# Blocks of 128 rows of an expert layer: seven products in pairs on the halves of the array

## The chip, the cores and the metric

The kernel runs on one core of one Trainium2 chip. A core has TensorE (PE, matrix products; PEld are its weight loads), VectorE (DVE), ScalarE (ACT), GpSimd (POOL), SyncE (SP) and 16 DMA engines. The metric is device time in microseconds (us) of one execution. All operands are float32. The trace shows two matmuls and two weight loads for each float32 matmul that the program writes.

## What is computed

Attention with a causal window of 64 on 8 batches of 8 heads, 576 rows and 64 columns, gives 4608 rows x of 512. Each row then goes through one of eight experts, chosen from its logits and its local gate:

```python
for b in range(B):
    prev_e = -1
    for s in range(S):
        fresh_e = int(np.argmax(logits[b, s]))
        if s == 0 or local_gate[b, s] < 0.5:
            e = fresh_e
        else:
            e = prev_e if prev_e >= 0 else fresh_e
        prev_e = e
        ls = logits[b, s] - logits[b, s].max()
        p = np.exp(ls)
        p /= p.sum() + 1e-09
        h = np.maximum(x[b, s] @ w1[e], 0.0)
        out[b, s] = p[e] * (h @ w2[e])
```

An expert has w1 of 512 x 1024 and w2 of 1024 x 512. How many rows an expert gets depends on the data.

## The kernel before

The attention comes first, and its rows go to a DRAM table; the first matmul of an expert (L1514) stands at 134.2 us of the profile. Routing gives each row a place in a block that belongs to one expert. There are four kinds of block: big ones of 256 rows (two slots of 128), small ones of 128 (one slot), halves of 64 and quarters of 32. `run` (L1590) works through a fixed list: three first blocks of 256, and then blocks 0 to 12 of 256 with four small ones behind blocks 1, 3, 5 and 7, a half one behind block 9, another at the end, and two quarters behind blocks 2 and 6. `more` (L1684) handles what is left over with other data.

A block has two layers. `hidden` (L1498) makes h = relu(x w1), transposed, `result` (L1534) makes y = h w2, times the row's probability. From the third of the first blocks on, every engine runs its instructions in the order in which the code writes them; nothing is rescheduled.

- **Plain form** (small, half, and quarter blocks). Small: `hidden` has 32 matmuls of 128x128 weights with 128 moving rows (L1514), in two groups of 512 columns, relu on ScalarE (L1527) and on VectorE (L1525). `result` has eight matmuls with 512 moving columns (L1566), one scaling copy on ScalarE (L1573), and a scatter of the rows by GpSimd. A half block has outputs of 64 columns, which go to the two halves of the array in turn (L1514, L1544).
- **Form of seven products** (big blocks). `big_hidden` (L1344) and `big_result` (L1398) cut both operands into 2 x 2 quarters. Seven products of quarters or of sums of quarters, added up, replace eight. VectorE makes the sums: `prepare` (L1294) four of x (tile `xs`, L1326) and four of w1 (`ws`, L1312); `prepare2` (L1333) four of w2 (`ws`, L1326); `halves` (L1338) four of h (`hs`, L1312). Three products of layer one are kept by ScalarE copies (`keep`, L1370); three adds on VectorE (L1375) and four relu on ScalarE (L1376) give the quarters of h. In layer two L1420 keeps, L1425 adds, L1447 scales the last quarter.

In `big_hidden` the products use three PSUM tiles `px`, `py`, `pz`; the fifth product's `px` is read by VectorE's second add, and the seventh product then goes on in `px`, so it has to wait for that add.

Order around a block i: weights for block i+2 and gathers of rows for block i+3 are asked for; `hidden(i)`, with `prepare2(i)` first on VectorE; `turn(i+1)` (L1268), which transposes the next block's x on VectorE (L1283) and, if the next block has the form of seven products, calls `prepare(i+1)`; `result(i)`, where the callbacks `hooks` put the rest of the next block's weight sums between its products. The tiles of sums exist once each (`bufs=1`), so `prepare2(i)` waits for the last product of `result(i-1)`. `pace` (L1194) ties each of GpSimd's gathers to a product. A block's last scatter is left for the next block (`late`). Two output tiles `y` are used in turn.

## Time and profile before

| | before |
|---|---|
| three runs | 626.38 us median (626.19 to 627.47) |
| profiled execution | 627.78 us |
| its span | 626.0 us |
| granted TensorE clock | 0.999 |
| DMA | 165.80 MB, mean 265 GB/s |

A profile's page has the busy time of each engine, and views group or list the instructions. In a row of the timeline stand start and length in us, engine, line, operation, output <- inputs, stationary or output shape, count, and in brackets how long the engine had been idle and what ended that. In a table of windows stand start:end, length, then for PE, PEld, DVE, ACT and POOL the busy time with the number of instructions, and at the end clock, DMA share and GB/s. A length counts to the result's arrival; instructions of one engine overlap, so that what each costs in a row is the distance of the starts.

### The profile page before, as it was taken

The numbers are of one execution on the slowest core, as the hardware profiler recorded it, in microseconds if no ns is written. First come the engines' busy times: TensorE is split into PE (matmuls) and PEld (weight loads), VectorE is DVE, ScalarE is ACT, GpSimd is POOL, SyncE is SP. The second block draws the span as 40 slices with busy tenths as digits, with TensorE's granted clock in tenths as the row PEclk, the third lists the DMA queues.
The fourth block names the chain that finished last, engine by engine and source line by source line (L and its number), as shares of the span: only waits on it lengthen the run. The fifth ranks groups of instructions, "written<-read, shape, count | busy, mean of one in ns | idle before, by whom it ended". The sixth has DMA issues, their size and how long they took to land. (4 is left out here: it accounts for less than half of the span.)

```text
span 626.0 us, 15072 instructions
## 1 busy us (share of the span) xinstructions
PE 600.5 (96%) x6253; PEld 528.9 (84%) x6253; DVE 403.2 (64%) x757; ACT 200.5 (32%) x368; POOL 271.4 (43%) x261
## 2 busy tenths in 40 slices
PE   7888988999999999999999999999999999999995
PEld 6677766788889999979899799978997998999994
DVE  6567579888996767347381885183926763886730
ACT  3766755722382232203130123112221322123120
POOL 4432111622102567437146775175275866452001
PEclk9999999999999999999999999999999999999999
DMA  8999998787945557476967866687768656955601
GB/s 328 401 415 407 365 378 284 273 304 250 385 153 186 190 210 281 170 272 246 394 245 259 321 198 217 230 314 300 299 239 316 256 189 223 403 193 208 233 18 40
DMA packets 31880, 165.80 MB, mean 265 GB/s; under 512 B 10531, under 2 KB 12217, under 8 KB 22586
## 3 DMA queue, kind: packets, MB, share of 16 engines
q1 hardware_dynamic: 20394, 135.54, 58.6%
q0 software_dynamic: 11408, 29.20, 13.0%
q8 instruction: 51, 0.84, 0.5%
q14 instruction: 27, 0.22, 0.1%
HBM read 145.52 MB, written 19.59 MB: 264 GB/s over the span
## 5 line engine op out<-in xcount | busy, mean ns | idle before, releaser
L1184 POOL DMA_INDIRECT xg<-xs,g x118 | 134.2, 1138 | 46.0 <-issue 25.3
L1494 POOL DMA_INDIRECT out_dram<-y,idx x36 | 41.1, 1142 | 161.3 <-DVE y L1425 68.5
L1414 PE MATMUL hp<-ws,hs 128*128 128x256 f32 x384 | 88.9, 380 | 0.0
L1414 PEld LDWEIGHTS hp<-ws,hs 128*128 128x128 f32 x384 | 72.5, 190 | 10.9 <-issue 1.2
L1363 PE MATMUL hp<-xs,ws 128*128 128x128 f32 x672 | 79.7, 275 | 0.0
L1363 PEld LDWEIGHTS hp<-xs,ws 128*128 128x128 f32 x672 | 77.3, 192 | 0.1
L1425 DVE SCALAR_TENSOR_TENSOR y<-hp,pws,kept 128x256 f32<-128x256 f32 x48 | 23.2, 482 | 68.2 <-issue 41.2
L1514 PE MATMUL hp<-xt,w 128*64 128x64 f32 (+2 forms) x640 | 66.2, 276 | 0.0
L1514 PEld LDWEIGHTS hp<-xt,w 128*128 128x128 f32 (+1 forms) x640 | 60.8, 170 | 4.1 <-issue 0.7
L1414 PE MATMUL hp<-w,h 128*128 128x256 f32 x256 | 60.5, 379 | 0.0
L1375 DVE TENSOR_TENSOR h<-hp,keep 128x512 f32<-128x512 f32 x42 | 28.6, 689 | 43.9 <-PE hp L1363 43.1
L1363 PEld LDWEIGHTS hp<-xt,w 128*128 128x128 f32 x448 | 53.2, 192 | 2.7 <-issue 2.3
L1363 PE MATMUL hp<-xt,w 128*128 128x128 f32 x448 | 54.7, 275 | 0.0
L394 PEld LDWEIGHTS sp<-w 64*64 64x64 f32 x1296 | 39.1, 135 | 16.2 <-issue 11.2
L1414 PEld LDWEIGHTS hp<-w,h 128*128 128x128 f32 x256 | 47.3, 190 | 5.7
L425 ACT ACTIVATE p<-sp 128x512 f32<-128x512 f32 x72 | 39.1, 596 | 37.1 <-PE sp L394 34.8
L440 PE MATMUL xo<-vb,p 128*64 128x74 f32 (+1 forms) x576 | 44.0, 228 | 6.9 <-DVE x L450 3.0
L394 PE MATMUL sp<-w 64*64 64x128 f32 (+1 forms) x1296 | 45.1, 267 | 5.7 <-issue 4.5
L430 DVE TENSOR_TENSOR p<-p,mask 128x1024 f32<-128x1024 f32 x29 | 35.8, 1235 | 22.4 <-ACT p L425 22.3
L1184 POOL DMA_INDIRECT pws<-xw,gx x40 | 44.3, 1107 | 13.2 <-issue 8.5
L440 PEld LDWEIGHTS xo<-vb,p 128*64 128x64 f32 x576 | 38.3, 136 | 12.6 <-issue 5.2
L1376 ACT ACTIVATE h<-h 128x512 f32<-128x512 f32 x42 | 26.3, 630 | 60.1 <-DVE h L1375 60.1
(287 smaller groups left out, 977.5 us busy)
## 6 DMA issues: line engine op xcount, KB each, us to landing
w<-in_w_dram SPq DMA_DIRECT2D x22, 2048.0 KB, 9.4
w<-in_w1t_dram SPq DMA_DIRECT2D x20, 2048.0 KB, 8.7
w<-in_kq_dram SPq DMA_DIRECT2D x17, 1024.0 KB, 11.2
w<-in_w_dram SPq DMA_DIRECT2D x24, 512.0 KB, 8.5
xs<-x POOLq DMA_DIRECT2D x9, 1024.0 KB, 5.9
va<-in_v_dram SPq DMA_DIRECT2D x5, 1184.0 KB, 7.5
vtt<-in_vt_dram SPq DMA_DIRECT2D x5, 1024.0 KB, 6.2
va<-in_v_dram SPq DMA_DIRECT2D x3, 1040.0 KB, 15.5
```

The costliest lines, as they stand in the source:

```text
L394: nc.tensor.matmul(sp[j][c * WIN:(c + 1) * WIN, a:b], lhsT=kt[h, hp, block * WIN:(block + 1) * WIN], rhs=qt[h, hp, a:b], start=not biased, ...
L425: nc.scalar.activation(p[:, j], sp[j], Act.Exp, scale=DH ** -0.5)
L430: masked.append(nc.vector.tensor_tensor(p, p, m.to_broadcast([P, 2, SC]), op=Alu.mult))
L440: nc.tensor.matmul(xo[par * WIN:(par + 1) * WIN, j, s * VW:s * VW + n], lhsT=p[:, j, b * WIN:(b + 1) * WIN], rhs=w[:, s, 2 * hp + j, :n], ...
L1184: return self.nc.gpsimd.indirect_dma_start(out=out, out_offset=None, in_=table[:rows, :], in_offset=bass.IndirectOffsetOnAxis(ap=idx, axis=0))
L1363: mm = nc.tensor.matmul(out[:, m, :], lhsT=a[:, kk, m * P:(m + 1) * P], rhs=b[:, kk, :], start=start and m + kk == 0, stop=stop and (m, kk ...
L1375: nc.vector.tensor_tensor(o, x, y, op=add)
L1376: nc.scalar.activation(o, x if y is None else o, Act.Relu)
L1414: mm = nc.tensor.matmul(out, lhsT=a[:, m, :], rhs=b[:, m, :], start=start and m == 0, stop=stop and m == FK // 2 - 1, skip_group_check=True)
L1425: nc.vector.scalar_tensor_tensor(o, x, pw[i], y2, Alu.mult, Alu.add)
L1494: return self.nc.gpsimd.indirect_dma_start(out=self.out[:, :], out_offset=bass.IndirectOffsetOnAxis(ap=st["idx"][:, s:s + 1], axis=0), in_ ...
L1514: mm = nc.tensor.matmul(hp[a, i, :], lhsT=st["w1"][:, kk, m * P:(m + 1) * P][:, a], rhs=st["xt"][:, kk, :n], start=(kk == 0), stop=(kk == ...
```

## The change

Small blocks now take the form of seven products in both layers. Quarters are 64 rows wide. In layer one each product is a chain of matmuls with 64 columns of weights, alternating between the array's two halves (output partitions 0 to 63 and 64 to 127). In layer two a new function, `small_result`, runs two products at a time, one on each half, each pair into a PSUM bank of its own. What is to be added across halves is moved by ScalarE copies; VectorE adds with 64 partitions. The probability is applied to the whole of y later, together with the scatter. For the block behind a small one, `turn` and `prepare` move from ahead of `result` into its callbacks.

```diff
@@ -1212,8 +1212,9 @@
             slots = range(2 * n, 2 * n + 2) if n < NB else range(SM0 + n - NB, SM0 + n - NB + 1)
             if n >= KINDS[2]:
                 slots = range(HF0 + n - KINDS[2], HF0 + n - KINDS[2] + 1)
-        st.update(x=[], slots=slots, idx=idx, rows=P, big=len(slots) == 2, fast1=len(slots) == 2 and n not in PLAIN1,
-                  fast2=len(slots) == 2 and n not in PLAIN2)
+        st.update(x=[], slots=slots, idx=idx, rows=P, big=len(slots) == 2, fast1=n < KINDS[1] and n not in PLAIN1,
+                  fast2=n < KINDS[1] and n not in PLAIN2)
+        st["wide"] = P if st["big"] else HF
         if n >= KINDS[2]:
             st.update(quarter=n - KINDS[2], rows=QR)
         elif n >= KINDS[1]:
@@ -1293,7 +1294,8 @@
 
     def prepare(self, st, rest=False):
 
-        st["xq"] = quarters(st["xt"], DK, BIG)
+        c = 2 * st["wide"]
+        st["xq"] = quarters(st["xt"][:, :, :c], DK, c)
         st["xt"] = self.right("xs", st["xq"])
         w = quarters(st["w1"], DK, F)
 
@@ -1327,8 +1329,9 @@
         return t1, t2, t3, t4
 
     def sums(self, name, a):
-        t = self.one.tile([P, 4, a[0][0].shape[1], a[0][0].shape[2]], F32, name=name)
-        return [t[:, i] for i in range(4)]
+        n, c = a[0][0].shape[1:]
+        t = self.one.tile([P, 4, n, max(c, P)], F32, name=name)
+        return [t[:, i, :, :c] for i in range(4)]
 
     def prepare2(self, st, marks=()):
 
@@ -1350,23 +1353,25 @@
 
         nc, add = self.nc, Alu.add
         a, s, b, t = st["wq"], st["ws"], st["xq"], st["xt"]
-        self.prepare2(st)
+        if st["fast2"]:
+            self.prepare2(st)
+        n, c = FK // 2, st["wide"]
         st["h"] = h = self.wk.tile([P, FK, BIG], F32, name="h", bufs=1)
-        st["hq"] = hq = quarters(h, FK, BIG)
-        n = FK // 2
-
-        pz, py, px = (self.ps_h.tile([P, n, P], F32, name="hp") for _ in range(3))
+        st["hq"] = hq = quarters(h[:, :, :2 * c], FK, 2 * c)
+
+        pz, py, px = (self.ps_h.tile([P, n, P], F32, name="hp")[:, :, :c] for _ in range(3))
 
         def product(out, a, b, start=True, stop=True):
             for m in range(n):
                 for kk in range(DK // 2):
-                    mm = nc.tensor.matmul(out[:, m, :], lhsT=a[:, kk, m * P:(m + 1) * P], rhs=b[:, kk, :],
-                                     start=start and m + kk == 0,
-                                     stop=stop and (m, kk) == (n - 1, DK // 2 - 1), skip_group_check=True)
+                    for f in range(0, P, c):
+                        mm = nc.tensor.matmul(out[f:f + c, m, :], lhsT=a[:, kk, m * P + f:m * P + f + c],
+                                              rhs=b[:, kk, :], start=start and m + kk == 0,
+                                              stop=stop and (m, kk) == (n - 1, DK // 2 - 1), skip_group_check=True)
             self.pace(mm)
 
         def keep(i, x):
-            o = self.one.tile([P, n, P], F32, name=f"keep{i}")
+            o = self.one.tile([P, n, P], F32, name=f"keep{i}")[:, :, :c]
             nc.scalar.copy(o, x)
             return o
 
@@ -1393,7 +1398,8 @@
         product(px, a[1][1], t[3], False)
         relu(hq[1][0], px)
         step()
-        self.halves(st)
+        if st["fast2"]:
+            self.halves(st)
 
     def big_result(self, st, hooks):
 
@@ -1449,6 +1455,64 @@
             self.late = lambda: self.scatter(st, 1, y[1])
         else:
             self.scatter(st, 1, y[1])
+
+    def small_result(self, st, hooks):
+
+        nc, add = self.nc, Alu.add
+        hooks = iter(hooks)
+
+        def hook():
+            next(hooks, lambda: None)()
+
+        a, s, b, t = st["ha"], st["hs"], st["w2q"], st["w2t"]
+        w, lo, hi = D // 2, slice(HF), slice(HF, P)
+        r3, r2, r1 = (self.ps_h.tile([P, D], F32, name="hp")[:, :w] for _ in range(3))
+        r4 = self.ps_y.tile([P, D], F32, name="yp")[:, :w // 2]
+        y = self.wk.tile([P, D], F32, name="y")
+        u, v, g = (self.one.tile([P, w], F32, name=f"kept{i}") for i in range(3))
+
+        def both(out, *pairs):
+            for m in range(FK // 2):
+                for part, (x, z) in zip((lo, hi), pairs):
+                    mm = nc.tensor.matmul(out[part], lhsT=x[:, m, :], rhs=z[:, m, :], start=m == 0,
+                                          stop=m == FK // 2 - 1, skip_group_check=True)
+            self.pace(mm)
+
+        def plus(o, x, z):
+            nc.vector.tensor_tensor(o, x, z, op=add)
+
+        both(r1, (a[0][0], b[0][0]), (a[0][1], b[1][0]))
+        nc.scalar.copy(g[lo], r1[hi])
+        nc.scalar.copy(u[lo], r1[lo])
+        plus(y[lo, :w], u[lo], g[lo])
+        hook()
+        both(r2, (s[1], t[1]), (s[2], t[2]))
+        plus(v[lo], r2[lo], u[lo])
+        nc.scalar.copy(y[hi, w:], r2[hi])
+        nc.scalar.copy(g[hi], v[lo])
+        hook()
+        both(r3, (s[3], b[1][1]), (s[0], t[0]))
+        nc.scalar.copy(g[lo], r3[hi])
+        plus(v[hi], y[hi, w:], g[hi])
+        plus(y[hi, w:], r3[hi], v[hi])
+        plus(v[lo], v[lo], g[lo])
+        plus(y[lo, w:], r3[lo], v[lo])
+        hook()
+        both(r4, (a[1][1], t[3][:, :, w // 2:]), (a[1][1], t[3][:, :, :w // 2]))
+        nc.scalar.copy(u[hi, :w // 2], r4[lo])
+        plus(y[hi, :w // 2], r4[hi], v[hi, :w // 2])
+        plus(y[hi, w // 2:w], u[hi, :w // 2], v[hi, w // 2:])
+        for _ in range(3):
+            hook()
+
+        def store():
+            nc.scalar.activation(y, y, Act.Copy, scale=st["pw"][0])
+            return self.scatter(st, 0, y)
+
+        if st.pop("later", None):
+            self.late = store
+        else:
+            store()
 
     def quarter(self, st):
 
@@ -1534,7 +1598,7 @@
     def result(self, st, step, hooks=()):
         nc = self.nc
         if st["fast2"]:
-            return self.big_result(st, hooks)
+            return (self.big_result if st["big"] else self.small_result)(st, hooks)
         if "half" in st:
 
             s, w = st["half"], D // 2
@@ -1670,6 +1734,12 @@
             if i + 1 == len(order):
                 self.result(jobs[i], step)
                 continue
+            if jobs[i]["fast2"] and not jobs[i]["big"]:
+                after, left = jobs[i + 1], []
+                self.result(jobs[i], step, ((lambda: self.turn(after, False, True)),
+                                            (lambda: left.append(self.prepare(after, True))),
+                                            (lambda: None), (lambda: left.pop()())))
+                continue
             more = self.turn(jobs[i + 1], i + 1 < FB, rest=i + 1 >= FB and jobs[i]["fast2"])
             if i + 2 < FB and jobs[i + 1]["fast1"]:
                 self.prepare(jobs[i + 1])
```

The order of VectorE's instructions from the first of layer two's sums of a small block to its h, where before only the plain form's relu stood (in `h`, `xs`, `hs`, `y` and `w` the names above; `ws` with a number is one buffer of weight sums, `hp` a PSUM tile, `kept` and `keep` ScalarE's copies). Before, from the big block's last add to the transposes for the block behind:

```order
L1425 SCALAR_TENSOR_TENSOR y<-hp,pws,kept_3524 128x256
L1525 TENSOR_SCALAR h<-hp 128x4x128
L1283 STREAM_TRANSPOSE xt<-xg 128x4x4x32 x2
L1326 TENSOR_TENSOR xs<-xt 128x256
L1326 TENSOR_TENSOR xs<-xt,xs 128x256
```

Now, VectorE from the same add on:

```order
L1431 SCALAR_TENSOR_TENSOR y<-hp,pws,kept_3532 128x256
L1328 TENSOR_TENSOR ws_3570<-w 128x1024
L1328 TENSOR_TENSOR ws_3570<-w,ws_3570 128x1024
L1328 TENSOR_TENSOR ws_3570<-w 128x1024
L1328 TENSOR_TENSOR ws_3570<-w,ws_3570 128x1024
L1380 TENSOR_TENSOR h<-hp,keep_3596 128x4x64
L1380 TENSOR_TENSOR h<-hp,keep_3617 128x4x64
L1380 TENSOR_TENSOR h<-hp,keep_3636 128x4x64
L1314 TENSOR_TENSOR hs<-h 128x4x64
L1314 TENSOR_TENSOR hs<-hs,h 128x4x64
L1314 TENSOR_TENSOR hs<-h 128x4x64
L1314 TENSOR_TENSOR hs<-h,hs 128x4x64
```

One relu has become four weight sums, three adds and four sums of h. Behind them, VectorE in layer two of the same small block, where the transposes and sums for the next block now stand between the adds of this one:

```order
L1482 TENSOR_TENSOR y<-kept_3723,kept_3725 64x256
L1284 STREAM_TRANSPOSE xt<-xg 128x4x4x32 x2
L1482 TENSOR_TENSOR kept_3724<-hp,kept_3723 64x256
L1328 TENSOR_TENSOR xs<-xt 128x256
L1328 TENSOR_TENSOR xs<-xt,xs 128x256
L1328 TENSOR_TENSOR xs<-xt 128x256
L1328 TENSOR_TENSOR xs<-xt,xs 128x256
L1314 TENSOR_TENSOR ws_3758<-w 128x1024
L1314 TENSOR_TENSOR ws_3758<-ws_3758,w 128x1024
L1482 TENSOR_TENSOR kept_3724<-y,kept_3725 64x256
L1482 TENSOR_TENSOR y<-hp,kept_3724 64x256
L1482 TENSOR_TENSOR kept_3724<-kept_3724,kept_3725 64x256
```

The first add, which has to wait for two ScalarE copies, stands ahead of the transposes; three more adds follow the last row, then the next block's third and fourth weight sums of layer one, then its `prepare2`. TensorE at the same place, before:

```order
L1514 MATMUL hp<-xt,w 128x128 x32
L1566 MATMUL yp<-w,h 128x512 x8
L1363 MATMUL hp<-xt,w 128x128 x8
```

and now:

```order
L1368 MATMUL hp<-xt,w 64x64 x16
L1368 MATMUL hp<-xs,ws_3507 64x64 x32
L1368 MATMUL hp<-xt,w 64x64 x16
L1368 MATMUL hp<-xs,ws_3507 64x64 x16
L1368 MATMUL hp<-xt,ws_3507 64x64 x16
L1368 MATMUL hp<-xs,w 64x64 x16
L1477 MATMUL hp<-w,h 64x256 x8
L1477 MATMUL hp<-ws_3570,hs 64x256 x8
```

The 40 matmuls have become 112 of layer one and 32 of layer two; the first pair of layer two (L1477) reads h alone, and both its products stand ahead of everything that uses `hs`.

## The prediction

> **What bounds the kernel now.** I read the page's head first, then the windows of one block of 128 rows and the block behind it, then TensorE's timeline there.
>
> ```profile
> span 626.0 us, 15072 instructions
> PE 600.5 (96%) x6253; PEld 528.9 (84%) x6253; DVE 403.2 (64%) x757; ACT 200.5 (32%) x368; POOL 271.4 (43%) x261
> 336.03:350.05 14.02, 14.02 (x82) 10.19 (x81) 6.57 (x10) 1.07 (x2) 9.29 (x9) 1.00 0.85 315
> 350.05:374.64 24.59, 24.59 (x170) 23.14 (x168) 19.43 (x26) 6.35 (x11) 18.81 (x17) 1.00 0.69 240
> ```
>
> The reader is to see that TensorE (first figure after the length) is busy for the whole of both stretches at full clock. So TensorE sets the end, and a microsecond taken from it or put into it there is a microsecond of the kernel. VectorE (third) uses 6.57 of 14.02 us in the small block but 19.43 of 24.59 in the big one behind it.
>
> ```profile
> 267.96 7.31 PE L1514 MATMUL hp<-xt,w 128*128 128x128 f32 x64
> ...
> 336.03 7.31 PE L1514 MATMUL hp<-xt,w 128*128 128x128 f32 x64
> 343.18 7.03 PE L1566 MATMUL yp<-w,h 128*128 128x512 f32 x16
> 350.05 1.95 PE L1363 MATMUL hp<-xt,w 128*128 128x128 f32 x16
> ...
> 360.76 1.95 PE L1363 MATMUL hp<-xs,w 128*128 128x128 f32 x16
> 362.55 1.89 PE L1414 MATMUL hp<-w,h 128*128 128x256 f32 x8
> ...
> L1566 PE MATMUL yp<-w,h 128*128 128x512 f32 x64 | 28.1, 592 | 0.0
> ```
>
> Spacing is read from start to start. The small block takes 343.18 - 336.03 = 7.15 us for layer one and 350.05 - 343.18 = 6.87 us for layer two, 14.02 in all. In the big block behind it six products take 360.76 - 350.05 = 10.71 us (1.785 each) before the seventh. Four blocks of 128 rows run (64 matmuls of L1566 in all, 16 in each), the first from 267.96, each with a big block behind it.
>
> **The change, TensorE alone.** The blocks of 64 rows already run the new form, pairs of 64 columns on the halves:
>
> ```profile
> 528.77 1.89 PE L1414 MATMUL hp<-ws,h 128*128 128x256 f32 x8
> 530.59 3.95 PE L1514 MATMUL hp<-xt,w 128*64 128x64 f32 x128
> 534.37 3.63 PE L1544 MATMUL yp<-w,h 128*64 128x256 f32 x32
> 537.93 2.05 PE L1363 MATMUL hp<-xt,w 128*128 128x128 f32 x16
> 539.82 3.74 PE L1363 MATMUL hp<-xs,ws 128*128 128x128 f32 x32
> ```
>
> One 64-wide matmul costs 3.78 us / 128 = 29.5 ns, one 256-wide 3.56 us / 32 = 111 ns. The trace counts two matmuls for each of the program's (64 for 32 above), so layer one becomes 7 products of 32, 0.945 us each, 6.61 us; layer two becomes three pairs of products of 16 x 111 ns = 1.78 us, and a fourth pair of 16 matmuls 128 wide. That last form has no row; it lies between 29.5 and 111 ns, and I take the straight line, 57 ns, 0.91 us (ends 0.47 and 1.78). Sum 6.61 + 6.25 = 12.86 us against 14.02: **1.16 us less** per block, if nothing waits.
>
> The switch between full and half array is visible: 530.59 comes 0.09 us after 528.77 plus the product's usual 1.73, and the first product after it takes 1.89 for 1.79. I take 0.1 us on each side.
> [...]
>
> **VectorE and ScalarE.** Now the block needs sums of quarters, in place of plain operands. Prices:
>
> ```profile
> 343.38 0.69 DVE L1525 TENSOR_SCALAR h<-hp 128x512 f32<-128x512 f32 x1 [8.32 <-PE hp L1514]
> 343.98 1.29 DVE L1283 STREAM_TRANSPOSE xt<-xg 128x512 f32<-128x512 f32 x2
> 345.31 0.42 DVE L1326 TENSOR_TENSOR xs<-xt 128x256 f32<-128x256 f32 x1
> 345.77 0.42 DVE L1326 TENSOR_TENSOR xs<-xt,xs 128x256 f32<-128x256 f32 x1
> 346.11 0.42 DVE L1326 TENSOR_TENSOR xs<-xt 128x256 f32<-128x256 f32 x1
> 346.78 1.22 DVE L1312 TENSOR_TENSOR ws<-w 128x1024 f32<-128x1024 f32 x1
> 351.45 1.22 DVE L1326 TENSOR_TENSOR ws<-w 128x1024 f32<-128x1024 f32 x1
> 354.98 1.22 DVE L1326 TENSOR_TENSOR ws<-w,ws 128x1024 f32<-128x1024 f32 x1
> 357.46 0.69 DVE L1375 TENSOR_TENSOR h<-hp,keep 128x512 f32<-128x512 f32 x1 [1.26 <-PE hp L1363]
> ```
>
> Before, VectorE idles 8.32 us in the small block, and everything for the next block is done ahead: two transposes 1.33 us, four input sums 1.47 (345.31 to 346.78), four weight sums of layer one 4.67, four of layer two 4.75 (to 356.20). It is free 1.26 us before the next block's fourth product. So the margin is 1.3 us, and the change puts in: four weight sums of each layer (9.4 us), four sums each of x and h, three adds, and eight adds of the result.
>
> The first part is hidden. The small block's x sums and layer-one sums (about 5.7 us) fall into the big block ahead, where VectorE waits:
>
> ```profile
> 331.11 0.48 DVE L1425 SCALAR_TENSOR_TENSOR y<-hp,pws,kept 128x256 f32<-128x256 f32 x1 [4.57 <-issue]
> 334.57 0.48 DVE L1425 SCALAR_TENSOR_TENSOR y<-hp,pws,kept 128x256 f32<-128x256 f32 x1 [1.26 <-PE hp L1414]
> ```
>
> Without that cover they would cost their length; with it only the last y there comes some 1 us later, at the small block's start. The rest isn't hidden. I follow it with t = 0 at the block's first matmul, with these handovers and small pieces:
>
> ```profile
> 374.84 1.23 DVE L1326 TENSOR_TENSOR ws<-w 128x1024 f32<-128x1024 f32 x1 [0.25 <-PE hp L1414]
> 320.72 1.88 DVE L1375 TENSOR_TENSOR h<-hp,keep 128x512 f32<-128x512 f32 x3
> 321.44 1.83 ACT L1376 ACTIVATE h<-h 128x512 f32<-128x512 f32 x3 [4.31 <-DVE h L1375]
> 322.05 2.05 PE L1363 MATMUL hp<-xs,w 128*128 128x128 f32 x16 [0.24 <-DVE h L1375]
> 614.04 0.42 DVE L1525 TENSOR_SCALAR h<-hp 128x256 f32<-128x256 f32 x1 [3.20 <-PE hp L1514]
> L1466 ACT ACTIVATE qh<-yp 128x256 f32<-128x256 f32 x1 | 0.4, 383 | 1.4 <-PE yp L1462 1.4
> ```
>
> VectorE begins 0.20 us after TensorE passes to the next block (374.84 against 374.64, the window's end), an engine sees another's end some 0.04 us later, and 256 elements take 0.42 on VectorE, also out of PSUM, started 0.36 apart (0.46 where one needs the one before), and 0.38 on ScalarE. No row has adds of 64 partitions, or of 4 x 64 strided elements: from half that (if fewer partitions cost less) to half as much again; I take the 256-element rows, the nearest.
>
> Layer one: the layer-two sums run from 0.20 to 4.95; products three and four end at 2.9 and 3.9, so VectorE is late already. Its adds: 4.95 to 5.37, 5.30 to 5.72; the seventh product, which overwrites the second one's source, may start at 5.8, just when the sixth ends. It ends at 6.74, ScalarE's relu of it at 7.35. The first pair of layer two needs this last quarter at once (in the big form the first product does not): **about 0.5 us of wait**. TensorE finishes the first pair at 7.35 + 15 x 0.111 = 9.02. Then two copies on ScalarE (9.22 to 9.94) and VectorE's first add at 9.98; it had finished the four h sums at 8.45 and stands idle meanwhile, because the transposes for the next block are queued behind that add.
>
> From there VectorE never rests: add 0.38 (10.36), transposes 1.33 (11.69), add 0.38 (12.07), x sums 1.48 (13.55), two weight sums 2.4 (15.95), four adds 1.64 and two of 128 elements 0.48 (18.07), two weight sums 2.33 (20.40), four sums of layer two 4.75 (25.15), and the next block's adds, first 25.15 and second 25.75 to 26.44. TensorE ends its pairs at 10.80, 12.58, 13.49, starts the next block at 13.59 with the switch, and is ready for its seventh product at 13.59 + 10.71 = 24.30. That product overwrites what the second add reads: it waits until 26.48, **2.2 us**. Weight sums needed earlier are in time: the first by 14.8 for 15.4, the second by 15.95 for 17.2, the third by 19.3 for 20.7. Behind the waiting seventh product stands the whole layer two; from there on VectorE has its usual lead again (its h sums end 2.1 us after layer two begins, as now).
>
> Before, the same seventh product starts at 14.02 + 10.71 = 24.73. So 26.48 - 24.73 = **+1.75 us** per block, and four times that is +7.0. SyncE's weight loads keep their releases within half a microsecond, and GpSimd's gathers lead by three blocks; I cost both at nothing.
>
> One wait is new: the first add writes a buffer that the big block's first scatter reads.
>
> ```profile
> 267.27 1.01 POOL L1494 DMA_INDIRECT out_dram<-y,idx  x1 [6.26 <-DVE y L1425]
> 276.67 1.01 POOL L1494 DMA_INDIRECT out_dram<-y,idx  x1 [5.52 <-DMA out_dram<-y,idx]
> 338.41 1.02 POOL L1494 DMA_INDIRECT out_dram<-y,idx  x1 [0.30 <-issue]
> 344.55 1.01 POOL L1494 DMA_INDIRECT out_dram<-y,idx  x1 [2.60 <-DMA out_dram<-y,idx]
> ```
>
> The next scatter waited for the first to land, at 276.67 and 344.55. From the blocks' starts at 267.96 and 336.03 that is t = 8.7 and 8.5; the first of these scatters had waited for the last y, and with y 1 us later it lands at 9.7. The add comes at 9.98: covered, with 0.3 us to spare. Where it isn't, VectorE's queue moves by as much; up to 1 us per block goes into the upper end.
>
> The profiled execution is the span of 626.0 plus 1.8 around it, 627.78, 1.40 above the median of the runs shown; 627.78 + 7.0 = 634.8 stands for a median of 626.38 + 7.0 = **633.4 us**.
>
> **Rivals.** (a) VectorE is in time. Ten operations of the queue behind the first pair (9.02 to 26.44, 17.4 us) have no row of their own: two copies of 0.36 and eight adds, 2.9 us. At half price they give 1.8 us, and the change breaks even (it does from 1.75); from 2.2 us on TensorE sets the end, the block gives 24.30 - 24.73 = -0.43, four times -1.7: 624.7. For it: no row has these forms. Against it: 12 us of the queue are sums and transposes that have rows, and the page's short operations (0.42 for 256 elements, 0.69 for 512) show a fixed part of 0.15 that doesn't halve. Chance 0.09, with 0.05 for landing between and within 0.2%, which is about what a measurement can tell from no change (1.25 us).
> (b) The halves do not overlap in layer two, where each has its own weights and its own moving rows. Then a 256-wide matmul costs 0.216 (L1414's 1.73 / 8), layer two some 12.2 us, the seventh product starts at 7.35 + 12.2 + 0.1 + 10.71 = 30.4, +5.6 per block: 648.9. Against it: L1544 has two moving streams and goes at 111 ns. Chance 0.03.
> (c) The scatter lands late in each block, by 2 us after the add's time: +8 more, 641. Chance 0.06.
>
> **How the numbers follow.** The forecast keeps 0.77: +7.0 with the lone unknowns (the 128-wide pair -0.4 to +0.9 per block, but hidden behind VectorE; adds 1 us either way; scatter up to +1) gives 629 to 638. The range 628.5 to 640 leaves out (a) with what lies between it and the forecast, and (b), (c): not quite 2 in 10. Faster by over 0.2% 0.09, within 0.05, slower 0.86.
>
> **What would show it.** The steps, each for four blocks: 64x64 matmuls spaced 29.5 ns and 64x256 111 ns; a gap of about 0.5 us before the first pair of layer two, ended by ScalarE; VectorE without a pause from the first add to the next block's adds; a gap of 2 us before the seventh product of the next block, ended by VectorE's add (now L1380); 13.6 us from a small block's first matmul to the next block's. Wrong if that gap is missing, if the small block itself takes over 14, or if a wait sits elsewhere, as before the second product or at the scatter.

## The result, and the profile after

| | before | after |
|---|---|---|
| time, us (median; lowest to highest) | 626.29 (625.63 to 627.47) | 642.69 (640.20 to 646.11) |
| the profiled execution, us | 627.78 | 642.25 |
| its span, us | 626.0 | 640.5 |
| mean granted clock | 0.999 | 0.991 |

The kernel is slower: ratio 1.0263, 95% interval 1.0213 to 1.0314, or +16.4 us on the median. The prediction had +7.0 and a range of 628.5 to 640.0: the right side, and a time above the range. Ratios, here and below, compare executions in the faster of two states that the cores show; medians and spans are over all that ran.

First the page's head after the change, then the rows of the view of waits in which TensorE waits in the blocks of 128 rows and behind them (total us, times, longest):

```profile
span 640.5 us, 16918 instructions
PE 603.0 (94%) x7085; PEld 535.6 (84%) x7085; DVE 464.9 (73%) x861; ACT 216.2 (34%) x416; POOL 277.2 (43%) x261
...
PE hp L1368 <- DVE h L1380: 9.5, 6, 2.3
PE hp L1368 <- issue: 3.3, 2, 1.7
PEld hp L1477 <- ACT h L1381: 2.1, 4, 0.6
```

TensorE was busy for 96% of the span and is now for 94%: waits have come in. The first row is the predicted one (L1380 is VectorE's add); the third is the predicted half microsecond before the first pair of layer two. The second, "issue", is ended by nothing that the profile shows, and nobody had forecast it.

TensorE's timeline of the second block of 128 rows and the big block behind it answers to the rows of 336.03 to 360.76 shown of before:

```profile
339.01 1.15 PE L1368 MATMUL hp<-xt,w 128*64 128x64 f32 x32
339.99 2.04 PE L1368 MATMUL hp<-xs,ws 128*64 128x64 f32 x64
341.86 1.10 PE L1368 MATMUL hp<-xt,w 128*64 128x64 f32 x32
...
345.59 2.38 PE L1477 MATMUL hp<-w,h 128*64 128x256 f32 x15
...
352.44 2.05 PE L1368 MATMUL hp<-xt,w 128*128 128x128 f32 x16
354.33 3.74 PE L1368 MATMUL hp<-xs,ws 128*128 128x128 f32 x32
...
361.48 1.95 PE L1368 MATMUL hp<-xt,ws 128*128 128x128 f32 x16
365.69 3.42 PE L1368 MATMUL hp<-xs,w 128*128 128x128 f32 x16 [2.26 <-DVE h L1380]
```

The block takes 352.44 - 339.01 = 13.43 us (predicted 13.59, before 14.02), and one product of the new layer one 0.94 us. Then the six products run as ever, and the seventh, which would be ready at 361.48 + 1.79 = 363.27, starts at 365.69: 2.42 us late, of which the row counts 2.26 as idle, since a length runs to the result's arrival. This wait, ended by VectorE, is there in this form behind all four blocks. That product takes 3.42 us, not 2.05.

The first block of 128 rows shows the "issue" wait, in the middle of its last product of layer one:

```profile
270.88 0.74 PE L1368 MATMUL hp<-xs,w 128*64 128x64 f32 x17
273.23 0.62 PE L1368 MATMUL hp<-xs,w 128*64 128x64 f32 x14 [1.60 <-issue]
```

Every operand of that product is ready, since 17 of its matmuls have run. The fourth block has such a wait of 1.70 us; the second and third have none. Layer one takes 8.50 and 8.49 us in the first and fourth block, for 6.58 in the second.

**Where the 14.5 us of span went.** From a small block's first matmul to the seventh product behind it, the four blocks take 28.64, 26.68, 26.78 and 28.58 us, 110.68 in all; before, 4 x 24.73 = 98.92. That is +11.76, of which 3.83 are the two "issue" waits (3.3 us idle; 3.83 by the lengths of layer one) and 7.93 the predicted kind (7.0 forecast). The seventh product and the next one take 5.27, 5.26, 3.61 and 5.28 us for 3.52, **+5.3 us**. Together +17.1, less 2.8 because this execution reached its first small block 2.8 us sooner (265.18, before 267.96): 14.3 of 14.5. Those 2.8 us are luck, in a part that the change doesn't touch; other traces of a calm chip get there at 266.76 to 267.94.

For the slow products I read the granted clock. The windows below are cut to 3.41 us, and to a grid on which the stretches at half clock lie: those begin at 294.44, 366.12 and 506.07, and the distances, 71.68 and 139.95 us, are 21 and 41 times 3.413. Columns: length, busy time of TensorE, its weight loads, VectorE, ScalarE and GpSimd, then the clock, the DMA share and GB/s.

```profile
291.03:294.44 3.41, 1.15 (x10) 0.96 (x10) 3.30 (x5) 1.24 (x3) 2.84 (x2) 1.00 0.24 82
294.44:297.85 3.41, 3.41 (x16) 3.23 (x16) 2.10 (x4) 1.19 (x2) 2.50 (x4) 0.50 0.17 48
362.71:366.12 3.41, 1.15 (x10) 0.96 (x9) 3.38 (x5) 1.05 (x2) 2.80 (x3) 1.00 0.14 38
366.12:369.53 3.41, 3.41 (x17) 3.32 (x16) 2.10 (x4) 1.16 (x3) 2.50 (x4) 0.50 0.20 66
427.57:430.98 3.41, 2.94 (x27) 2.75 (x25) 3.38 (x4) 0.00 (x0) 2.80 (x3) 1.00 0.11 13
430.98:434.39 3.41, 1.62 (x14) 1.62 (x15) 2.68 (x5) 1.82 (x3) 2.80 (x3) 1.00 0.16 55
434.39:437.80 3.41, 3.41 (x19) 3.05 (x19) 3.00 (x9) 1.07 (x2) 2.50 (x4) 1.00 0.75 233
502.66:506.07 3.41, 1.23 (x11) 1.23 (x12) 2.69 (x4) 1.83 (x3) 2.80 (x3) 1.00 0.27 96
506.07:509.48 3.41, 3.41 (x14) 2.96 (x13) 3.27 (x6) 0.60 (x1) 2.80 (x3) 0.50 0.44 101
```

Behind a stretch in which TensorE was busy for 1.15, 1.15 or 1.23 us, the next runs at half clock. In the third block the same wait falls across a border of the grid, TensorE is busy for 2.94 and 1.62 us in the two stretches, and the clock stays at 1.00. So the wait costs its own length and, when it falls badly, some 1.75 us more.

### The profile page after: what moved, and what is told of

Its sections match the earlier page's. It is cut to its first block, busy times and chain, and to the rows that moved or that the text cites. A ratio compares the mean times of both kernels' runs of the same rounds, so it can differ in the third digit from the quotient of the medians.

```text
span 640.5 us, 16918 instructions
## 1 busy us (share of the span) xinstructions
PE 603.0 (94%) x7085; PEld 535.6 (84%) x7085; DVE 464.9 (73%) x861; ACT 216.2 (34%) x416; POOL 277.2 (43%) x261
## 3 DMA queue, kind: packets, MB, share of 16 engines
q0 software_dynamic: 11408, 29.20, 12.9%
## 5 line engine op out<-in xcount | busy, mean ns | idle before, releaser
L1184 POOL DMA_INDIRECT xg<-xs,g x118 | 138.4, 1173 | 42.4 <-issue 25.6
L1368 PE MATMUL hp<-xs,ws 128*128 128x128 f32 (+1 forms) x1056 | 92.3, 256 | 0.0
L1368 PEld LDWEIGHTS hp<-xs,ws 128*128 128x128 f32 (+1 forms) x1056 | 89.2, 172 | 0.1
L1368 PE MATMUL hp<-xt,w 128*128 128x128 f32 (+1 forms) x704 | 64.1, 257 | 0.0
L1368 PEld LDWEIGHTS hp<-xt,w 128*128 128x128 f32 (+1 forms) x704 | 61.0, 172 | 2.8 <-issue 2.4
L1380 DVE TENSOR_TENSOR h<-hp,keep 128x512 f32<-128x512 f32 (+1 forms) x54 | 32.5, 627 | 33.6 <-PE hp L1368 33.5
L1381 ACT ACTIVATE h<-h 128x512 f32<-128x512 f32 (+1 forms) x54 | 30.7, 583 | 77.4 <-DVE h L1380 77.4
L1184 POOL DMA_INDIRECT pws<-xw,gx x40 | 46.3, 1157 | 13.6 <-issue 8.9
L1328 DVE TENSOR_TENSOR ws<-w 128x1024 f32<-128x1024 f32 x40 | 49.0, 1228 | 3.8 <-PE hp L1420 2.5
L1328 DVE TENSOR_TENSOR ws<-w,ws 128x1024 f32<-128x1024 f32 x40 | 49.0, 1224 | 0.7
L394 PE MATMUL sp<-w 64*64 64x128 f32 (+1 forms) x1296 | 42.8, 263 | 4.9 <-issue 3.0
```

The source lines that it names most:

```text
L394: nc.tensor.matmul(sp[j][c * WIN:(c + 1) * WIN, a:b], lhsT=kt[h, hp, block * WIN:(block + 1) * WIN], rhs=qt[h, hp, a:b], start=not biased, ...
L1184: return self.nc.gpsimd.indirect_dma_start(out=out, out_offset=None, in_=table[:rows, :], in_offset=bass.IndirectOffsetOnAxis(ap=idx, axis=0))
L1328: self.nc.vector.tensor_tensor(o, x, y, op=sub)
L1368: mm = nc.tensor.matmul(out[f:f + c, m, :], lhsT=a[:, kk, m * P + f:m * P + f + c], rhs=b[:, kk, :], start=start and m + kk == 0, stop=sto ...
L1380: nc.vector.tensor_tensor(o, x, y, op=add)
L1381: nc.scalar.activation(o, x if y is None else o, Act.Relu)
```

## The experiments

The kernels of one set ran on one chip, each beside the kernel before, and are compared only with what ran there. The chips of the first, second, third and fifth set ran the kernel before in 637.7 to 647.6 us (medians), with waits that the page of before doesn't have, and the changed kernel, where it ran, at ratios of 1.038 to 1.048; the text calls them restless. Only the chip of the fourth set was as calm as that of the result (627.45).

Theory A: VectorE's queue makes the wait, and the wait the halved clock. Rival: the waits that no engine ends (theory B, later theories F and G on their cause) make most of the loss.

### First set: take the wait away, and make one in the old kernel

The changed kernel with the work for the next block at the head of `small_result`, ahead of the adds of the result:

```diff
@@ small_result
+        hook()
+        hook()
         both(r1, (a[0][0], b[0][0]), (a[0][1], b[1][0]))
 ...
         plus(y[lo, :w], u[lo], g[lo])
-        hook()
         both(r2, (s[1], t[1]), (s[2], t[2]))
 ...
-        hook()
```

> The changed kernel with the next block's transposes, x sums and first two weight sums ahead of the small block's adds. Theory (VectorE's queue makes TensorE wait 2.26 us before the seventh product of the next block, and that idle time is what halves the clock afterwards): VectorE's 1.5 us of idle time ahead of the first add goes, the wait shrinks to some 0.7 to 0.9 us, the clock stays at 1.00, and the time falls by 4 x 1.5 + 5.3 = about 11 us against the changed kernel, to some 631. Rival (the clock is lost for a reason that has nothing to do with the wait, such as the switch to half the array or the load of 64-wide matmuls): the wait shrinks, the clock is still lost, about 637. Stalls of 1.7 us inside the 64-wide products, put down to issue, stay in both.

The changed kernel with matmuls that nobody reads, where TensorE would wait (in the big blocks behind the small ones):

```diff
+        if st.get("fill"):
+            spare = self.ps_y.tile([P, D], F32, name="yp")[:, :2 * P]
+            for _ in range(5):
+                nc.tensor.matmul(spare, lhsT=a[1][1][:, 0, :P], rhs=st["w1"][:, 0, :2 * P], start=True, stop=True)
```

> The changed kernel with five matmuls of 256 columns that nobody reads (2.16 us) ahead of the seventh product of each big block behind a small one. Theory (the idle time halves the clock): TensorE has no gap there any more, the seventh product starts where it did (26.7 us after the small block's first matmul), runs in 1.8 us and not 3.1, the clock stays at 1.00 and the time falls by some 5 us, to 637. Rival (the products behind the wait are slow from contention with VectorE or from the 64-wide forms): they stay at 3.1 and 2.2 us, the time stays at 642.

The kernel before with sums that nobody reads on VectorE, in the big blocks behind the small ones, four and five of them:

```diff
+        for _ in range(st.get("extra", 0)):
+            spare = self.one.tile([P, FK // 2, D // 2], F32, name="spare")
+            self.nc.vector.tensor_tensor(spare, w2[0][0], w2[0][1], op=Alu.add)
```

> The kernel before, with four more sums of 128x1024 on VectorE behind the layer-two sums of each big block behind a small one; their result is not used. Four sums are 4.7 us against a margin of 3.2 us at the seventh product: theory, a wait of 1.4 to 1.5 us there in four blocks, no loss of clock, +6 us, 632. Rival (any wait of over a microsecond costs the clock): +6 and up to 1.7 us for each of four, 636 to 639.

> The same with five sums, 5.85 us: a wait of 2.6 us in four blocks. Theory (a wait of some 2.3 us and more halves the clock for 3.4 us in most of the cases): 4 x 2.6 plus 3 or 4 times 1.7 = 15.5 to 17.5 us more, 642 to 644, the granted clock of 0.50 for 3.4 us behind the wait. Rival (the clock loss belongs to the 64-wide forms, which this kernel doesn't have in these blocks): +10.5, 637, clock 1.00.

Measured: e1_reorder 661.85 us, ratio 1.0296 (1.0205 to 1.0387); e2_fill 670.23, 1.0460 (1.0378 to 1.0543); e3_old_4_sums 651.42, 1.0164 (1.0057 to 1.0272); e4_old_5_sums 650.66, 1.0152 (1.0056 to 1.0248). Two rows of the waits of e1_reorder (667.71 us in its profiled execution, the longest of its four) say what became of it:

```profile
PE hp L1368 <- issue: 16.8, 17, 5.8
...
PE hp L1368 <- DVE h L1380: 0.7, 3, 0.3
```

With the work moved, the wait for VectorE falls from 2.26 us to 0.3 at most, and in both e1_reorder and e2_fill the seventh product runs at full clock in all four places (1.8 to 1.9 us to the next product's start). That much theory A expected. But TensorE also came late to these places, by other waits, so the reordering isn't shown here to be the whole reason. A cleaner case is the second place in the later sets: the unaltered kernel waits 2.28 us there in e9_after_third, e16_after_fourth and e18_less (none in e6_after_again), the reordered one 0.90 and 0.91 in e12_reorder_again and e17_reorder_third.

The time does not follow: 631 and 637 us were expected of e1_reorder and e2_fill. That was a miss, and it gave the second question. Of the 16.8 us of "issue" waits in e1_reorder only 6.2 stand inside 64-wide products; 10.3 stand in two places in 128-wide ones, before the third product of the big blocks behind the first and the third small one (e2_fill: 6.7 and 5.6 of 12.4). The first of the two, and ScalarE at the same time:

```profile
294.19 3.78 PE L1368 MATMUL hp<-xs,ws 128*128 128x128 f32 x16 [4.48 <-issue]
...
293.55 0.59 ACT L1375 COPY keep<-hp 128x512 f32<-128x512 f32 x1 [4.05 <-remote]
```

The third product goes on in the PSUM tile that this copy reads, and it starts 0.05 us behind the copy's end (294.14). So this is a wait for ScalarE that the profile puts down to "issue"; ScalarE itself had stood still for 4.05 us, released by "remote", a semaphore whose sender the profile doesn't show. The other one (5.81 us, at 443.50) ends 0.05 us behind such a copy too, and so, within 0.06 us, do the longest waits in 128-wide products of e2_fill, e12_reorder_again, e16_after_fourth and e17_reorder_third (2.2 to 4.4 us). In the result's profiled execution ScalarE has no such stop.

The old kernel's form brings the clock's fall too. The seventh product at the third of the four places, with four sums and then with five (timeline):

```profile
436.46 2.05 PE L1366 MATMUL hp<-xs,w 128*128 128x128 f32 x16 [1.47 <-DVE h L1378]
```

```profile
436.81 3.25 PE L1366 MATMUL hp<-xs,w 128*128 128x128 f32 x16 [2.71 <-DVE h L1378]
```

and the grid's stretches with five sums, two at the third place and two at the fourth:

```profile
434.01:437.42 3.41, 0.70 (x6) 0.61 (x6) 3.31 (x5) 1.22 (x3) 2.58 (x3) 1.00 0.25 82
437.43:440.84 3.41, 3.41 (x16) 3.23 (x16) 2.07 (x4) 1.19 (x2) 1.69 (x3) 0.50 0.17 38
505.69:509.10 3.41, 2.05 (x19) 1.86 (x17) 3.34 (x3) 0.00 (x0) 2.58 (x3) 1.00 0.33 115
509.11:512.52 3.41, 2.02 (x17) 2.02 (x18) 2.68 (x6) 1.82 (x3) 1.89 (x2) 1.00 0.23 41
```

Four waits of 2.70 to 2.76 us: the one that lies in a single stretch of the grid (busy 0.70) halves the clock, the one that is split (2.05 and 2.02) doesn't, nor do the other two, and four waits of 1.44 to 1.47 never do. No 64-wide products run there, so they are not what brings the clock down. One case of four is fewer than the three or four expected, and the times don't show the price: the two kernels measured the same (651.42 and 650.66 us, two executions each, 632 and 642 to 644 expected), with more "issue" waits in e3_old_4_sums (2.1 us for 0.6). What a lost clock costs rests on the traces.

### Second set: is it the form, and is it the traffic

> The kernel before, profiled beside the others on the chip that this call gets. The chip of the first experiments needed 643 us for it, where 626 stood before: theory (late instruction fetches, seen as waits for issue and as ScalarE standing still without a semaphore), waits of this kind of 10 us and more on TensorE's way on such a chip, hardly any on one that needs 626. Rival (a lower clock or slower operations): the same operations are longer throughout.

> The changed kernel again. Theory: the wait before the seventh product of the big block behind each small one is 2.26 us again in all four places, the clock halves for 3.4 us behind some of them, and the waits for issue inside the 64-wide products come at other places and in other numbers than in the first profile, between 0 and 4 blocks, more of them where the kernel before is slow too. Rival (the waits for issue belong to fixed instructions): blocks one and four again, 1.6 and 1.7 us.

The changed kernel with SyncE's loads of the next block's layer-two weights held back until the last matmul of the small block's layer one:

```diff
+                if end:
+                    self.tc.add_manual_dep(d.ins, end.ins.name, ...
 ...
+            if i >= FB and small:
+                self.weights(jobs[i + 1], order[i + 1], ("w2", ), end=jobs[i]["end"])
+                self.weights(jobs[i + 2], order[i + 2])
```

> The changed kernel with the load of the next block's second weights (2 MB) held back until the small block's layer one is done, so that the DMA engines carry little beside gathers while the 64-wide products run. Theory (instruction fetches come late because the DMA engines are full): no wait for issue inside the 64-wide products, layer one in 6.6 us in all four blocks, 3 us less than the changed kernel where that has two such waits. Rival (the sequencer itself cannot keep up with 64-wide products): they stay.

Layer one by the change, layer two as before:

```diff
-                  fast2=n < KINDS[1] and n not in PLAIN2)
+                  fast2=len(slots) == 2 and n not in PLAIN2)
```

> Layer one of the small blocks in the new form, layer two as before. VectorE has no layer-two sums, h sums and adds to make there, so it is done with the next block's sums about 8 us after layer one ends. Theory: no wait before the next seventh product, clock 1.00, small block 6.6 + 6.9 + 0.2 = 13.7 us against 14.0, -1.3 in all, and waits for issue as in the changed kernel, 0 to 4 times 1.7, so 625 to 632 against 626. Rival (layer one alone already overloads VectorE): a wait of a microsecond or more before the next block's seventh product.

Measured: the kernel before once more, 640.45 us in one execution (median there 637.73); e6_after_again 666.95, ratio 1.0478 (1.0425 to 1.0531); e7_quiet 676.35, 1.0579 (1.0511 to 1.0648); e8_layer1 662.18, 1.0408 (1.0351 to 1.0465). In e5_before_again the clock (0.999) and the lengths of the operations are those of before (L1414: 1.89 us for eight matmuls in both timelines), so the chip's loss lies in waits; of "issue" waits in the expert blocks it has 3.4 us, not 10. The "issue" waits at L1368, the line of both forms, are 11.1, 7.1 (there L1371) and 10.7 us in the other three; 7.3, 6.4 and 8.6 of them stand in 64-wide products. In e7_quiet the DMA engines are nearly idle while the second block's layer one runs (from 351.22 us; share 0.20 from 350 to 364 us, 0.84 in e6_after_again in the same stretch), and the short waits are there in both, more of them in e7_quiet, so busy DMA engines are not their cause. e7_quiet also waits 11.6 us for ScalarE before layer two of the small blocks (0.6 in e6_after_again); ScalarE itself stood still there twice, 8.5 us in all, released by "remote", so it isn't shown that holding the weights back did it. Layer one alone keeps most of the loss.

### Third set: layer two alone, and the form alone in the old kernel

> The changed kernel once more, beside the next three on one chip. Theory A (VectorE's queue and the clock behind it): a wait for VectorE of about 2.2 us before the seventh product of each of the four big blocks, a granted clock near 0.5 for some 3.4 us behind most of them, 3.5 to 5.3 us in all lost by it; waits that no engine ends inside the 64-wide products add from 3 (first measurement) to 11 us (second) on top. Ratio to the kernel before 1.025 to 1.05.

```diff
-                  ... fast1=n < KINDS[1] and n not in PLAIN1,
+                  ... fast1=len(slots) == 2 and n not in PLAIN1,
```

> Layer two of the four blocks as changed, layer one as before: 128x128 matmuls, no 64x64 ones. Theory B (the waits that no engine ends belong to the 64-wide matmuls of layer one): they are gone, under 2 us in all. The rival (they belong to the whole stretch, whatever TensorE does there): 7 us or more, as in the changed kernel. VectorE's queue behind the first pair keeps its length, so both expect the wait of 2 to 3 us before the seventh product, and by theory A a granted clock near 0.5 behind it in some of the four. By A and B together: four times (2.5 us of wait, 0.7 of gain by layer two) is +7, with 0 to 7 for the clock: ratio 1.011 to 1.022. By the rival 1.025 or more.

The kernel before, layer one of the four blocks cut into 64x64 pieces (its values there then differ from the reference's; the amount of work is as told):

```diff
-                    for f in range(0, P, st["rows"]):
-                        a = slice(f, f + st["rows"])
-                        mm = nc.tensor.matmul(hp[a, i, :], lhsT=st["w1"][:, kk, m * P:(m + 1) * P][:, a],
-                                         rhs=st["xt"][:, kk, :n], ...
+                    c, z = (HF, HF) if n == P else (st["rows"], n)
+                    for f in range(0, P, c):
+                        for r in range(0, n, z):
+                            mm = nc.tensor.matmul(hp[f:f + c, i, r:r + z], lhsT=st["w1"][:, kk, m * P + f:m * P + f + c],
+                                             rhs=st["xt"][:, kk, r:r + z], ...
```

> The kernel before with layer one of its four blocks cut into 64x64 matmuls on the quarters of the array, 128 in the program where 32 were, and nothing else: no sums, no products by seven, no new wait. At 29.5 ns each of the 256 that the trace counts, layer one takes 7.55 us for 7.15: +0.4 per block, +1.6 in all, ratio 1.0026. Theory B (waits inside runs of 64-wide matmuls that no engine ends): these come here too, some 60 ns for each instruction in stretches, 5 to 15 us in all, ratio 1.01 to 1.025. If they stay away, the form alone doesn't bring them, and something beside it does (operands that VectorE has just made, or its own traffic).

> The changed kernel with the transposes, the input sums and the first two weight sums for the next block ahead of the adds of the small block's result, where VectorE stood still. By theory A the wait before the seventh product goes (below 0.4 us) and the clock behind it stays at 1.00: 4 x 2.26 + 4 x 1.5 = up to 15 us less than the changed kernel on the same chip, ratio to the kernel before 1.00 to 1.01. If the waits that no engine ends decide instead (theory B), the time moves by less than 5 us from the changed kernel's and these waits take 10 us or more.

Measured: e9_after_third 674.73, ratio 1.0411 (1.0348 to 1.0473); e10_layer2 652.06, 1.0102 (1.0036 to 1.0169); e11_old_quarters 655.12, 1.0133 (1.0076 to 1.0190); e12_reorder_again 674.39, 1.0347 (1.0267 to 1.0427).

Layer two alone has no "issue" waits in these blocks, and keeps the others: 2.30 and 2.41 us for VectorE before the seventh product in the second and fourth big block, with half clock behind each, 0.88 in the third, none in the first, and new ones of 1.91 and 1.12 us for ScalarE before a third product, and of 3.11 for VectorE in the big block ahead of the fourth. It gains nothing either: its blocks take 14.3 to 15.5 us, where layer one's values now leave through two engines and the first pair waits for them (for VectorE 1.8 us in the four blocks). The form alone, without sums or new order, brings "issue" waits into 64-wide products of the old kernel (11.0 us): theory B holds for these, not for the ones in 128-wide products, which e11_old_quarters doesn't have in layer one of the big blocks behind the small ones. e12_reorder_again is a second miss for A: the waits for VectorE before the seventh product are down to 1.6 us, and the ratio is not clear of that of e9_after_third (the intervals overlap), where up to 15 us less had been expected. On this chip TensorE lost so much earlier in the blocks that VectorE was in time at some places anyway (4.3 us of waits for it in e9_after_third, 9.5 in the result).

### Fourth set, on a calm chip: the rate of instructions, and GpSimd

The same edit over halves only, so 64 columns of weights by 128 moving columns:

```diff
+                    c = HF if n == P else st["rows"]
+                    for f in range(0, P, c):
+                        mm = nc.tensor.matmul(hp[f:f + c, i, :], lhsT=st["w1"][:, kk, m * P + f:m * P + f + c],
+                                         rhs=st["xt"][:, kk, :n], ...
```

> The kernel before with layer one of its four blocks cut over the halves only: 64 columns of weights, 128 moving columns, 64 matmuls in the program where 32 were and e11_old_quarters had 128; nothing else. If the waits that no engine ends come from the rate at which TensorE takes its instructions (theory B), half the rate leaves little of them: below 4 us in the four blocks, layer one 7.2 to 7.6 us, ratio to before below 1.006. If they come from any use of the array's parts, or from the stretch itself, they stay near the 14 us of e11_old_quarters and the ratio is 1.01 or more.

e11_old_quarters with one gather for a block:

```diff
-            if st["plain"]:
+            if n < KINDS[1]:
                 asks.append((x, self.xs, gx[:, s:s + 1], rows))
```

> e11_old_quarters with one gather of whole rows on GpSimd for each block of 128 rows, where four gathers of quarter rows were (the rows then stand in another order in the block, so what layer one is given differs; the work of TensorE, VectorE and ScalarE is the same). If GpSimd's backlog of gathers, which is longest in the second and fourth block, is what the 64-wide matmuls meet (theory G), their waits fall from 14 to below 4 us and the ratio from 1.013 to below 1.005. If not, 8 us or more remain, and the two worst blocks stay the second and the fourth.

> e11_old_quarters once more, on the chip of the two runs above: ratio 1.007 to 1.02, waits that no engine ends inside its 64-wide matmuls of 8 to 16 us. Below 5 us here would say that they belong to the chip, and the two runs above can then tell nothing.

Measured: e13_old_halves 627.00 us, ratio 0.9999 (0.9972 to 1.0026); e14_one_gather 636.25, 1.0134 (1.0089 to 1.0180); e15_quarters_again 636.33, 1.0126 (1.0068 to 1.0184). Layer one of the first and third block in the timeline of e13_old_halves:

```profile
266.76 7.21 PE L1514 MATMUL hp<-xt,w 128*64 128x128 f32 x128
...
398.36 7.21 PE L1514 MATMUL hp<-xt,w 128*64 128x128 f32 x128
```

and in e15_quarters_again:

```profile
267.94 6.34 PE L1515 MATMUL hp<-xt,w 128*64 128x64 f32 x209
276.03 1.62 PE L1515 MATMUL hp<-xt,w 128*64 128x64 f32 x47 [1.75 <-issue]
...
402.58 4.93 PE L1515 MATMUL hp<-xt,w 128*64 128x64 f32 x160
410.42 4.41 PE L1515 MATMUL hp<-xt,w 128*64 128x64 f32 x96 [2.91 <-issue]
```

The same work in half as many instructions runs without a wait; in twice as many it stops (6.5 us in all, less than the 8 to 16 expected, at the expected ratio). The 4.41 us of the last row hold a clock halved from 410.10 on, behind a wait that no VectorE ended. TensorE stops behind 209 matmuls in the first block, 160 in the third and 214 in the fourth. e14_one_gather stops behind the same 209, 160 and 214, with GpSimd busy for 171.0 us instead of 269.2, so theory G falls, though its waits (5.5 us) are below the 8 us that had been named for that. e11_old_quarters, on another chip, stopped behind 209 and 160 too. A wait that stands at a place in the instruction stream, whatever the chip and the traffic, points to the stream itself: theory F, TensorE's instructions arrive late. The DMA view lists instruction packets (q8 is a queue; in the page after the change 58 packets and 0.95 MB, 16 KB each). In the changed kernel's first measurement a single one of 16 KB starts between 268 and 274 us, in the window from 270.84 to 270.86 (packets, MB, share of the 16 engines in that window):

```profile
q8 instruction: 1, 0.02, 292.5%
```

| kernel, place | TensorE's last matmul | the packet, from to | TensorE goes on | behind the landing |
|---|---|---|---|---|
| after, first block | 271.40 | 270.85 to 271.79 | 273.23 | 1.44 |
| after, fourth | 481.03 | 480.58 to 481.57 | 482.95 | 1.38 |
| e15_quarters_again, first | 274.06 | 273.68 to 274.56 | 276.03 | 1.47 |
| e15_quarters_again, third | 407.29 | 408.18 to 409.12 | 410.42 | 1.30 |
| e15_quarters_again, fourth | 482.17 | 481.80 to 482.72 | 484.18 | 1.46 |
| e16_after_fourth, first | 276.76 | 276.41 to 277.35 | 278.64 | 1.29 |

Each wait ends 1.3 to 1.5 us behind the landing of one 16 KB packet, which started within 0.9 us of TensorE's last matmul. The places can be counted in the traces, with the queue's semaphore instructions. From the first to the third block's wait of e15_quarters_again TensorE's queue runs 2560 instructions (1265 matmuls, 1266 weight loads, 29 semaphores), and 1536 from there to the fourth block's; the two waits of the changed kernel lie 4096 apart: exactly 5, 3 and 8 times 512. And in every trace that has the first block's wait, of the old kernel and of the changed one, it stands behind the 7617th instruction of that queue.

### Fifth set: the two causes together

e16_after_fourth is the changed kernel and e17_reorder_third is e1_reorder, unaltered. e18_less was to leave out one sum:

```diff
+            if NB <= n < KINDS[1]:
+                jobs[i + 1]["less"] = 1
             more = self.turn(jobs[i + 1], i + 1 < FB, rest=i + 1 >= FB and jobs[i]["fast2"])
```

> The changed kernel, as the measure for the next two on one chip. Theory A: a wait for VectorE of 2.2 to 2.3 us before the seventh product of all four big blocks, and the granted clock halved for 3.4 us behind those whose TensorE idle time in one stretch of the clock's grid (3.41 us) is above 1.9 us, at full behind those below 1.85. Theory F (instruction fetch): waits of 1.3 to 1.9 us inside the 64-wide products of the first and the fourth block, at the same matmuls as in the first measurement (after 17 of the seventh product's, and in the sixth product), each ending 1.3 to 1.6 us behind the landing of a 16 KB instruction packet. Ratio 1.02 to 1.03 on a chip as calm as the first.

> The changed kernel with the transposes, the input sums and two weight sums for the next block ahead of the adds of the small block's result. Theory A: waits for VectorE's add before the seventh product at most 0.4 us, clock 1.00 behind them, so 4 x 1.9 to 2.26 + 3.5 to 5.3 = 11 to 14 us less than e16_after_fourth on this chip: ratio to before 1.000 to 1.007. Theory F: TensorE's instructions are the same, so the waits for instructions stay where they are. The rival (only the waits that no engine ends count): no more than 4 us less than e16_after_fourth.

> The changed kernel with the last of the four layer-two weight sums left out in the big block behind each small one (the third stands in its place, so those blocks' results differ). VectorE's queue is 1.19 us shorter there: theory A expects the wait before the seventh product at 2.26 - 1.19 = 1.05 to 1.1 us in all four, too short for the clock: 1.00 behind all four. So 4 x 1.19 + 3.5 to 5.3 = 8 to 10 us less than e16_after_fourth. The rival for the clock (the 64-wide products bring it down, not the wait) expects 0.50 behind the waits as before and only 4 to 5 us less.

Measured: 668.78 us, ratio 1.0376 (1.0282 to 1.0470); 671.10, 1.0441 (1.0338 to 1.0543); 672.17, 1.0424 (1.0320 to 1.0529). The edit of e18_less stands behind a branch that these blocks don't take, so VectorE runs the same 861 instructions, and the run is only one more of the changed kernel: a failed experiment, and the direct test of a shortened wait was not made. The wait behind the 17th matmul of the first block's seventh product is in all three (1.65, 1.49 and 1.70 us), as theory F expected, and in every other run whose layer one has the new form (in e8_layer1 behind the 16th, at the same count of the queue) but e7_quiet, where the packet lands at 278.77, before TensorE gets there. The wait in the fourth block, which theory F expected too, is in none of the three. e17_reorder_third is the third miss for A on a restless chip: only one wait for VectorE is left there that is longer than half a microsecond (0.91 us), e16_after_fourth has only one (2.28 us), and 14.5 and 12.9 us of "issue" waits at L1368, about half of them (7.8 and 6.8) in 128-wide products, hide the rest.

## Why the prediction came out too low

**Right, by its own steps.** The products of layer one take 0.94 us each for 0.945 forecast. The first pair waits for ScalarE, 2.1 us over four blocks, forecast 0.5 each. VectorE's first add of the result starts 10.06 us into the second block for 9.98, and from there it runs without a pause to the next block's adds:

```profile
349.07 0.42 DVE L1482 TENSOR_TENSOR y<-kept,kept 64x256 f32<-64x256 f32 x1 [1.73 <-ACT kept L1486]
349.41 1.29 DVE L1284 STREAM_TRANSPOSE xt<-xg 128x512 f32<-128x512 f32 x2
...
363.10 1.22 DVE L1328 TENSOR_TENSOR ws<-w,ws 128x1024 f32<-128x1024 f32 x1
364.35 1.89 DVE L1380 TENSOR_TENSOR h<-hp,keep 128x512 f32<-128x512 f32 x3
```

The seventh product starts 26.68 and 26.78 us into the second and third block, forecast 26.48, and 26.72 and 26.67 into the first and fourth when the "issue" waits are taken off. That is 0.2 to 0.3 us a block too late, 0.9 in all: the sum's small prices were that far off. In all four places the wait is ended by the add that was named, and where the reordering could be compared, at the second place, it is shorter (0.9 us for 2.28), so its cause is the one named. Rival (a), VectorE in time, and (b), halves that don't overlap, are out; so is (c), since no wait for the scatter stands before that add, only ScalarE's 1.73 us.

**Wrong, first: the step from one block's loss to four times it.** The prediction counted the wait at its own length, +1.75 a block, and let everything behind it run at the usual pace, "from there on VectorE has its usual lead again". VectorE had; the clock hadn't. Three of the four waits lie in one stretch of the clock's grid and are followed by half clock (0.50) for the next 3.41 us: **+5.3 us**. That of the third block is split and costs nothing more. e4_old_5_sums shows the same in a kernel without the change (busy for 0.70 us of a stretch, the next at 0.50). Why the clock falls there, and what sets the grid, no run shows. The page before had no such case, since no wait of TensorE's in its expert blocks comes near this length (the longest is 0.4 us); the clock at 1.00 in its windows was taken for granted.

**Wrong, second: the step "TensorE alone".** 29.5 ns for a 64-wide matmul came from a run of 128 of them (530.59), in which the DMA view of before has no instruction packet. In layer one there are now 224 traced matmuls where 64 were, and in the first and the fourth block TensorE stands there for 1.6 and 1.7 us, until 1.44 and 1.38 us behind the landing of an instruction packet: **+3.8 us** in the first measurement, by the lengths of layer one. That fetch is the cause of these two waits is inferred from their places (the 7617th instruction of the queue in the first block, 4096 from there to the fourth), from the packets' landings, and from the half rate, without such a wait in e13_old_halves; no run changed the fetch itself. Why the packet starts so late, and why some blocks have none, was not tried.

Without either one of the two the time would have been inside the range (642.69 - 5.3 = 637.4, or - 3.8 = 638.9). The range was also narrower than its own chances: what it leaves out, (a) with what lies next to it, (b) and (c), adds up to 0.23, not to under 2 in 10.

**Left open.** On the restless chips there are also waits of 0.2 to 0.4 us, one for each six matmuls or so, in the second and fourth block, and single ones of 1 to 5 us. Of e6_after_again:

```profile
347.20 0.75 PE L1368 MATMUL hp<-xt,w 128*64 128x64 f32 x19
348.14 0.39 PE L1368 MATMUL hp<-xt,w 128*64 128x64 f32 x6 [0.20 <-issue]
348.87 0.45 PE L1368 MATMUL hp<-xt,w 128*64 128x64 f32 x7 [0.34 <-issue]
```

From 348.14 to 348.87, six matmuls take 0.73 us, 0.12 each for 0.03. In e7_quiet eight such waits (0.19 to 0.46 us) stand between 351 and 359 us, and the DMA view of that stretch has no instruction packet. They are most in 64-wide products, but not only there: e3_old_4_sums has six of them (2.1 us) in the plain form's 128-wide matmuls. Full DMA engines are not their cause (share 0.20 in e7_quiet); what is, these runs don't say. Of the single ones, those of 2.2 to 5.8 us in 128-wide products are waits for ScalarE, as above, and what ScalarE waits for is open. The profiled execution of the result has none of either. What the changed kernel would take without the wait for VectorE on a calm chip wasn't measured: e1_reorder ran on restless ones only. No version here beat the kernel before; e13_old_halves equals it.

## What to carry to other kernels

A wait of TensorE's is priced with the clock behind it: a single one that left it busy for 1.2 us of a stretch of 3.41 or less cost half of the next stretch as well (5.27 us for 3.52), and where four waits of 2.7 us were placed in the old kernel, the grid split three of them and they cost nothing more. Where a change trades fewer columns for more and smaller matmuls, count instructions as a resource beside the array's time: what runs at 29.5 ns apiece for 4 us need not do so for 7. And where work is taken from the engine that sets the end and given to one with idle time, follow the second engine's queue to the point where the first waits for it: here a lead of 1.3 us didn't pay for 9.4 us of sums.

## What the runs showed of the hardware

- Each stretch at half clock in the windows above is 3.41 us long, and the three of the changed kernel begin 71.68 and 139.95 us apart, 21 and 41 times 3.413 us. On that grid, across these traces, where TensorE made one pause, 1.79 us idle in a stretch or less left the clock at 1.00 (1.44 to 1.47 in e3_old_4_sums, 1.75 and 1.79 in e15_quarters_again, 1.79 in the third block after), and 2.18 us or more (after: 2.18 and 2.26; e4_old_5_sums: 2.71; e10_layer2: 2.30; e15_quarters_again: 2.59) halved it for the next. Between these it went both ways: 1.92 in e10_layer2 left it, 1.80 in e18_less halved it. With many short waits in a stretch less was enough (1.27 us in sum from 347.54 in e17_reorder_third, 1.60 from 438.12 in e16_after_fourth), so idle time as the profile counts it doesn't settle it alone.
- An instruction packet of 16 KB takes 0.88 to 0.99 us in the table's rows, and TensorE, idle for 1.6 to 2.9 us there, goes on 1.3 to 1.5 us behind its landing. The places lie 2560 and 1536 instructions of the queue apart in e15_quarters_again and 4096 after the change; the first block's wait stands at the same one, the 7617th, in ten of the eleven runs with the new layer one.
- A 128-wide matmul on a half takes 7.14 us / 128 = 56 ns (e13_old_halves, 266.76 to layer two's start at 273.90), 1.9 times the 64-wide one's 29.5: layer one over halves costs what it costs on the whole array, 7.14 and 7.15 us.
